# Attention into a spectral layer: early weights loaded as row pairs of two modes, and the spectrum moved on PE's queue

## The chip, the cores and the metric

The kernel runs on one core of one Trainium2 chip. A core has a matrix engine (TensorE, "PE" in the profile, its weight loads "PEld"), three engines for element-wise work (VectorE "DVE", ScalarE "ACT", GpSimd "POOL"), a synchronising engine (SyncE, "SP") and 16 DMA engines that move data between HBM and the on-chip memory SBUF. Each engine works through a queue of its own in order and waits at semaphores. Matmul results go to a second memory, PSUM, which is divided into banks.

The metric is the device time of one execution in microseconds (us), as a median of several runs.

## What is computed

The first half is causal attention with a decay that comes from a gate `f`; the second a layer that multiplies the first 64 Fourier modes of the sequence by complex matrices, adds the result back, and applies a channel matrix with a ReLU. Cut to the core:

```python
scores = (q @ k.T) / sqrt(64) + cum[:, None] - cum[None, :]   # cum = cumsum(log(clip(f)))
attn   = softmax(where(causal, -1e9, scores))
x      = concat_heads(attn @ v)                # [8, 576, 512]
X      = rfft(x, axis=1)[:, :64]
Yr     = Xr @ w_r[m] - Xi @ w_i[m]             # for each mode m, [512, 512] matrices
Yi     = Xr @ w_i[m] + Xi @ w_r[m]
u      = x + irfft(Y, n=576)
out    = u + relu(u @ w_ch)
```

Batch 8, 8 heads of 64 channels, sequence 576. The two weight tensors hold 64 x 512 x 512 float32 numbers each, 134 MB in all; DMA reads them as float32 and writes them to SBUF as bfloat16.

## The kernel before

**Two stages.** Attention runs over 32 pairs of heads, `pairs[i] = (g, b)`: g (0 to 3) is a block of 128 channels, b the batch. The loop at L588 makes 34 passes; each issues loads for pairs ahead and then interleaves pair i's scores with pair i - 1's product with v and pair i - 2's Fourier transform. The main loop (L835) then goes over 16 units u of four modes each and finishes the product with the mode matrices; inverse transform, channel matrix and stores follow. The order of the instructions is the order in which the code emits them: nothing reorders them.

**A pass of the attention loop** on PE: scores in three tiles (L457, bank `sps`), v's transposes (`turn_v`, L404, tile `tv`), products with v of the pair before (`av`, L505, `pav`), transposes of q and k of the next pair (L377, `tp`), a last score block whose exponential is `e` (L451), the last block of `av`, v's transposes back (`back_v`, L415, `vp`), then the Fourier transform `dft` of pair i - 2 (L536 or L557, `pd`). ACT takes the exponentials `et` (L464), the copy `vs` of v (L426) and the copies out of `pd`. DVE copies transposed q, k and v (L382, L406), normalises (`rcp` L519, `x_all` L520), applies masks (L470, L473, `m` L474) and scales v for the next pair (`vn`, L394). Setup work is emitted in passes 0 to 9: the Fourier basis `bas3` in pass 1 (`setup_basis`), small constants in pass 2 (`setup_late`), the inverse basis in 3 to 9 (`bip`).

**Units and blocks.** A unit's weights for one block `dc` of input channels are 1 MB in bfloat16. Blocks are loaded in the order `wseq` (L128): blocks 0 and 1 of units 0 to 7 (`by_rows`, 16 of them), block 0 of units 8 to 15, block 1 of units 8 to 11, and the rest in the main loop. For `by_rows` a block holds w_r and w_i of 128 channels, one row of 512 numbers in a packet. For the other units a block holds w_r (dc = 0) or w_i (dc = 1) of 256 channels as row pairs, 1024 numbers in a packet. Blocks live in seven buffers of `wpool` and, for seven of them, as guests in parts of `x_all` and `yx` that are free then (L136). Attention issues half blocks, two in a pass and one in passes 3, 6, 9, 12 and 15 (`less`). 28 blocks are used within attention (`spec_early`): two in each of passes 10 to 13 and 17 to 19, one in each of 20 to 33. A block's use is `spec_mms`: eight matmuls of 512 columns into one bank `A`. There, four modes stand side by side in four groups of 32 output columns of PE (rows 32j of `A`). The result is copied to `yacc` by ACT (block 0) or added by DVE (block 1).

**Spectrum.** `dft` multiplies x of pair i (576 rows in four blocks of 128 and one of 64) by `bas3` with three copies c of the basis (-imaginary, real, imaginary). For g < 2, the modes below 32 go to `XS`, 24 numbers (c, b) for each mode, all 128 channels; the modes from 32 go to `XQ` for even and odd channels, in the half of partitions that belongs to g. That is three groups of five matmuls and two copies on ACT. For g of 2 or 3 two groups of five write `XP`.

**Loads.** Weights, q, k and v are issued from POOL's queue (L112, L122, L167, L176, L185), stores from SP's. A load waits for its buffer and for the landing of the load that was issued eight loads before on this queue.

## Time and profile before

| | |
|---|---|
| median of 3 runs | 437.46 us (435.47 to 437.74) |
| the profiled execution | 436.07 us, span 434.2 us |
| granted TensorE clock, mean | 0.947 |
| PE busy | 360.4 us, 83% of the span |
| DVE busy | 265.7 us, 61% |
| ACT busy | 229.0 us, 53% |
| POOL busy | 141.0 us, 32% |
| DMA | 96.79 MB in 60,289 packets; 28,752 of them under 2 KB |
| HBM | 163.73 MB read, 9.44 MB written |

The profile is one execution; all its times count from the span's start. The page cuts the span into 40 equal slices (10.9 us each) and prints a digit for each engine, the busy share in tenths, 9 for 90% or more. GB/s counts the bytes written by DMA: a weight is read at 4 bytes and written at 2. The DMA share in a table of stretches is the sum of the packets' times over 16 engines, and packets overlap, so it stands above 1 when the engines are busy throughout. Recorded times of a matmul hold its way through the pipeline, so neighbours overlap: what a group costs PE is the time to the next group's start.

### The profile page before, as it was taken

How to read it: one execution, taken by the hardware profiler on the slowest of the kernel's cores; microseconds unless marked ns; L12 is line 12 of the kernel's file. 1: busy time of each engine (PE TensorE's matmuls, PEld its weight loads, DVE VectorE, ACT ScalarE, POOL GpSimd, SP SyncE). 2: the span in 40 equal slices, each digit the busy share in tenths (PEclk: the TensorE clock that was granted, in tenths of full speed). 3: DMA queues.
4: the chain of work that ended last, by engine and by line, in shares of the span. 5: the costliest groups of instructions: out<-in, count | busy, mean ns of one | idle time of the engine just before them, and what ended most of it. 6: DMA issues, size and time to landing. Idle time of an engine off the chain costs nothing.

```text
span 434.2 us, 10695 instructions
## 1 busy us (share of the span) xinstructions
PE 360.4 (83%) x4433; PEld 200.9 (46%) x4444; DVE 265.7 (61%) x651; ACT 229.0 (53%) x374; POOL 141.0 (32%) x211
## 2 busy tenths in 40 slices
PE   1699999988898899999986386599788599989993
PEld 1466666655665565665653133244343233334330
DVE  6687888776878797787785122222323157654794
ACT  4656667677775567667661022033313176652783
POOL 6544445434544434444304101111111112001273
PEclk9999999999999999999999579599969699999997
DMA  9999999999999999999999999999999999996598
GB/s 193 205 234 220 232 222 232 226 229 230 231 231 228 230 230 230 230 230 229 236 214 212 212 212 212 212 213 212 212 212 212 212 212 212 211 212 126 188 381 305
DMA packets 60289, 96.79 MB, mean 223 GB/s; under 512 B 3664, under 2 KB 28752, under 8 KB 60240
## 3 DMA queue, kind: packets, MB, share of 16 engines
q0 software_dynamic: 54544, 85.63, 103.6%
q1 hardware_dynamic: 5696, 10.47, 6.7%
q8 instruction: 35, 0.57, 0.5%
q14 instruction: 14, 0.11, 0.1%
HBM read 163.73 MB, written 9.44 MB: 399 GB/s over the span
## 4 chain that ended last, share of the span: by engine, by line
DMA 49%; PE 31%; DVE 9%; ACT 5%; issue 3%; POOL 1%; DVEq 0%; ACTq 0%; POOLq 0%
DMA w<-in_moe_w_i_dram 34%; DMA w<-in_moe_w_r_dram 13%; PE pd L536 5%; PE pav L505 5%; PE sps L457 5%; DVE qkT L382 4%; PE tv L404 3%; ACT et L464 2%; PE A L221 2%; PE pd L557 2%; DVE vT L406 2%; PE tp L377 2%; DMA qk<-in_k_dram 2%; DVE x_all L520 2%; PE U L692 2%
## 5 line engine op out<-in xcount | busy, mean ns | idle before, releaser
L464 ACT ACTIVATE et<-sps 128x1024 bf16<-128x1024 f32 x96 | 93.2, 1023 | 11.6 <-PE sps L457 9.7
L505 PE MATMUL pav<-vs,et 128*128 128x65 bf16 (+1 forms) x896 | 51.3, 197 | 14.6 <-ACT e L451 14.3
L505 PEld LDWEIGHTS <-et 128*128 128x128 bf16 (+1 forms) x896 | 39.9, 103 | 34.0 <-issue 31.7
L382 DVE COPY qkT<-tp 128x640 bf16<-128x640 bf16 x64 | 48.9, 765 | 3.4 <-PE tp L377 3.4
L892 DVE TENSOR_TENSOR Yb<-A,yx 128x512 bf16<-128x512 f32 x15 | 10.4, 692 | 59.0 <-PE A L221 59.0
L406 DVE COPY vT<-tv 128x576 bf16<-128x576 bf16 x32 | 24.2, 757 | 35.4 <-PE tv L404 34.7
L732 PE MATMUL pxw<-wch,xT 128*128 128x512 bf16 (+1 forms) x152 | 41.1, 418 | 1.0 <-DVE xT L722 0.4
L457 PE MATMUL sps<-qkT 64*128 64x512 bf16 (+4 forms) x320 | 39.4, 310 | 1.3 <-DVE qkT L382 1.1
L426 ACT COPY vs<-vp 128x576 bf16<-128x576 bf16 x32 | 20.4, 639 | 37.1 <-PE vp L422 37.1
L520 DVE TENSOR_TENSOR x_all<-pav,rcp 128x384 bf16<-128x384 f32 (+2 forms) x96 | 36.2, 377 | 3.3
L221 PE MATMUL A<-w,XP 128*16 128x512 bf16 (+1 forms) x240 | 21.3, 435 | 20.2 <-DMA w<-in_moe_w_i_dram 12.1
L377 PE MATMUL tp<-ident_bf,qk 128*64 128x128 bf16 x576 | 30.1, 235 | 9.3 <-DMA qk<-in_k_dram 9.0
L185 POOL DMA_DIRECT2D w<-in_moe_w_r_dram x16 | 11.9, 743 | 74.6 <-PE A L221 69.2
L739 ACT CAST XW<-pxw 128x512 bf16<-128x512 f32 (+1 forms) x16 | 9.4, 585 | 45.2 <-PE pxw L732 45.2
L739 ACT CAST yx<-pxw 128x512 bf16<-128x512 f32 (+1 forms) x24 | 14.0, 585 | 33.9 <-PE pxw L732 33.9
L782 ACT CAST x_all<-pu 128x512 bf16<-128x512 f32 (+1 forms) x40 | 23.4, 585 | 13.1 <-PE pu L775 12.2
L112 POOL DMA_DIRECT2D qk<-in_q_dram x32 | 19.5, 609 | 30.8 <-PE tp L377 6.5
L185 POOL DMA_DIRECT2D w<-in_moe_w_i_dram x19 | 13.3, 698 | 50.0 <-PE A L221 40.5
L732 PEld LDWEIGHTS <-xT 128*128 128x128 bf16 (+1 forms) x160 | 15.8, 109 | 22.9 <-issue 9.6
L722 DVE COPY xT<-ptr 128x576 bf16<-128x576 bf16 x32 | 14.7, 458 | 17.8 <-PE ptr L717 17.0
L112 POOL DMA_DIRECT2D qk<-in_k_dram x32 | 19.2, 601 | 19.1 <-DMA w<-in_moe_w_i_dram 5.9
L377 PEld LDWEIGHTS <-qk 128*64 128x64 bf16 x576 | 19.5, 116 | 12.7 <-issue 8.2
(158 smaller groups left out, 703.3 us busy)
## 6 DMA issues: line engine op xcount, KB each, us to landing
w<-in_moe_w_i_dram POOLq DMA_DIRECT2D x19, 1024.0 KB, 31.9
w<-in_moe_w_r_dram POOLq DMA_DIRECT2D x16, 1024.0 KB, 29.9
w<-in_moe_w_r_dram POOLq DMA_DIRECT2D x23, 512.0 KB, 11.3
w<-in_moe_w_i_dram POOLq DMA_DIRECT2D x19, 512.0 KB, 11.0
out_dram<-o_sb SPq DMA_DIRECT2D x36, 256.0 KB, 2.8
vt<-in_v_dram POOLq DMA_DIRECT2D x29, 288.0 KB, 10.4
qk<-in_q_dram POOLq DMA_DIRECT2D x32, 144.0 KB, 10.7
qk<-in_k_dram POOLq DMA_DIRECT2D x32, 144.0 KB, 10.7
```

What stands on the lines that cost most here:

```text
L112: nc.gpsimd.dma_start(qk[64 * n : 64 * n + 64, :, :], src[b, 2 * g : 2 * g + 2, :, :].rearrange("h (p r) d -> p h (r d)", p=64),)
L185: nc.gpsimd.dma_start(w8[:, j : j + step, :, :].rearrange("p m r e -> p m (r e)"), src[m : m + step, 256:512, :].rearrange("m (p r) e -> p ...
L221: nc.tensor.matmul(A[32 * j : 32 * j + M, :], lhsT=lhsT, rhs=rhs, start=st_, stop=sp_)
L377: nc.tensor.transpose(tp[64 * hp : 64 * hp + 64, r - r0, :, :].rearrange("p n c -> p (n c)"), qk[:, hp, r * 64 : r * 64 + 64], ident_bf[:, :],
L382: nc.vector.tensor_copy(st[i]["T"][:].rearrange("p n (c r) -> p n c r", r=9)[:, :, :, r0:r1], tp[:, 0 : r1 - r0, :, :].rearrange("p r n c ...
L406: nc.vector.tensor_copy(st[i]["vT"][:].rearrange("p (c r) -> p c r", r=9), tv[:].rearrange("p r c -> p c r"))
L457: nc.tensor.matmul(ps[:, hp, c : c + n], lhsT=KT[sl, jb * 128 : jb * 128 + 128], rhs=QT[sl, i0 : i0 + n], start=True, stop=True,)
L464: nc.scalar.activation(st[i]["et"][:, T, :, :], ps[:], ACT.Exp, scale=scale)
L505: nc.tensor.matmul(pav[:Ms, sb % 3, hp, :], lhsT=eblk(i, hp, jb, sb), rhs=rhs, start=(jb == 0), stop=(jb == sb),)
L520: nc.vector.tensor_tensor(x_all[:ns, g, b, lo:hi, :].rearrange("p s (h d) -> p s h d", h=2), pav[:ns, lo % 3 : lo % 3 + n, :, 0:Dh], _stri ...
L732: nc.tensor.matmul(pxw[rows, :], lhsT=xT[:, eb, sb * 128 : sb * 128 + Ms], rhs=wch[:, eb, :], start=(eb == 0), stop=(eb == NEB - 1),)
L739: nc.scalar.copy(XW[to][rows, sb, :], pxw[rows, :])
```

## The change

Four things are done together.

1. The `by_rows` blocks are loaded as row pairs: partition 2p + h holds rows 2p and 2p + 1 of modes 4u + 2h and 4u + 2h + 1 (h is 0 or 1), w_r and w_i after one another, 1024 numbers in a packet. The other blocks of dc < 2 are loaded in two halves of 128 channels, into the even and the odd partitions; in the main loop, where a block was one load, it is now two (four blocks).
2. A `by_rows` block's eight matmuls go to two groups of 64 or 48 output columns instead of four of 32. Each multiplies the two modes of both partition parities at once; the spectrum holds zeros where the parity doesn't match. The spectrum of dc = 0 is `XS`, that of dc = 1 lies in a part of `yx`; in both the modes (16) are innermost, so that a matmul's stationary operand has a step of 16 elements.
3. `dft` for g < 2 takes x of all channels, of the channels moved by one up, and by one down (`x_pad` has 32 zeros ahead of x for it): three groups of five matmuls with 192, 48 and 144 columns (g = 1: 192, 144, 48) instead of 96 each. The copies: two on ACT with a factor per partition that is 1 or 0 by parity, 96 elements each; and `XQ` by one ACT copy of 192 elements for g = 0 (all partitions), by two additions on DVE for g = 1.
4. `dft(i - 2)` is emitted ahead of `back_v(i)` instead of after the first early unit.

`bas3` is written with its modes in another order, by nine instructions on DVE instead of three, with a reduction for the parity and eight memsets. Some constants (`m_i`, `m_f`, `rep`) move into `XP`'s place, and the guests in `yx` start at other offsets.

```diff
         if by_rows(u, dc):
             for t, src in enumerate((moe_w_r, moe_w_i)):
                 if half in (None, t):
                     nc.gpsimd.dma_start(
-                        w8[:, t, :, :],
-                        src[4 * u : 4 * u + 4, dc * 128 : (dc + 1) * 128, :].rearrange("m p e -> p m e"),
+                        w8[:, 2 * t : 2 * t + 2, :, :].rearrange("p k r e -> p k (r e)"),
+                        src[4 * u : 4 * u + 4, dc * 128 : (dc + 1) * 128, :].rearrange(
+                            "m (p r) e -> p m (r e)", r=2
+                        ),
                     )
         elif dc < 2:
             src = (moe_w_r, moe_w_i)[dc]
-            step = 4 if half is None else 2
-            for j in range(2 * (half or 0), 4 if half != 0 else 2, step):
-                m = 4 * u + j
-                nc.gpsimd.dma_start(
-                    w8[:, j : j + step, :, :].rearrange("p m r e -> p m (r e)"),
-                    src[m : m + step, 0:256, :].rearrange("m (p r) e -> p m (r e)", r=2),
-                )
+            for g in range(2):
+                if half in (None, g):
+                    nc.gpsimd.dma_start(
+                        w8[g:128:2, :, :, :].rearrange("p m r e -> p m (r e)"),
+                        src[4 * u : 4 * u + 4, 128 * g : 128 * g + 128, :].rearrange(
+                            "m (p r) e -> p m (r e)", r=2
+                        ),
+                    )
...
     def spec_mms(A, u, dc, first, last):
         w8 = wtile.pop((u, dc))
+        if by_rows(u, dc):
+            for t in (1, 0):
+                for r in range(2):
+                    for k in range(2):
+                        M = 64 if t else 48
+                        c0 = 16 * (56 * r + (0 if t else 8)) + 2 * u + k
+                        nc.tensor.matmul(
+                            A[64 * k : 64 * k + M, :],
+                            lhsT=by_mode(dc)[:, c0 : c0 + 16 * M - 15 : 16],
+                            rhs=w8[:, 2 * t + k, r, :],
+                            start=first and t == 1 and r == 0,
+                            stop=last and t == 0 and r == 1,
+                        )
+            return
...
     def dft(i):
         g, b = pairs[i]
         if g < 2:
-            pd = psM.tile([128, 3, 3, ML], F32, tag="m", name="pd")
-            half = slice(64 * g, 64 * g + 64)
-            for r in range(3):
+            pd = psM.tile([128, 3, 2 * NM], F32, tag="m", name="pd")
+            even, odds, upper = (16, 0, 32) if g == 0 else (48, 32, 0)
+            cut = 16 if g else 48
+            for o, m0, m1, at in (
+                (0, 0, NM, even),
+                (1, 0, cut, NM + even),
+                (-1, cut, NM, 0),
+            ):
                 for sc in range(NSB):
                     ns = SBLK[sc]
-                    xs = x_all[:ns, g, b, sc, :]
+                    M = 127 if o == 1 and sc == NSB - 1 else 128
+                    c0 = 32 + ((g * B + b) * NSB + sc) * 128 + o
                     nc.tensor.matmul(
-                        pd[half, r, :, :] if r else pd[:, 0, :, :],
-                        lhsT=xs[:, r - 1 : 128 : 2] if r else xs,
-                        rhs=bas3[:ns, sc, :, ML:NM] if r else bas3[:ns, sc, :, 0:ML],
+                        pd[:M, :, at : at + m1 - m0],
+                        lhsT=x_pad[:ns, c0 : c0 + M],
+                        rhs=bas3[:ns, sc, :, m0:m1],
                         start=(sc == 0),
                         stop=(sc == NSB - 1),
                     )
-            nc.scalar.copy(
-                XS[:, g, 0 : 24 * ML].rearrange("p (m c b) -> p c m b", c=3, b=8)[:, :, :, b],
-                pd[:, 0, :, :],
-            )
-            nc.scalar.copy(
-                XQ[half, :, :, :].rearrange("p r (c b) m -> p r c b m", c=3)[:, :, :, b, :],
-                pd[half, 1:3, :, :],
-            )
+            pr = pd[:].rearrange("p c (r m) -> p r c m", r=2)
+            for h, k in enumerate((even, odds)):
+                nc.scalar.activation(
+                    by_mode(g)[:, 0 : 16 * 112].rearrange("p (r c q) -> p r c q", r=2, q=16)[
+                        :, :, 32 * h + b : 32 * h + 24 : 8, :
+                    ],
+                    pr[:, :, :, k : k + 16],
+                    ACT.Copy,
+                    scale=odd[:, h : h + 1],
+                )
+            xq = XQ[:].rearrange("p r (c b) m -> p r c b m", c=3)[:, :, :, b, :]
+            up = pr[:, :, :, upper : upper + 32]
+            if g == 0:
+                nc.scalar.activation(xq, up, ACT.Copy, scale=odd[:, 0:1])
+            else:
+                for r in range(2):
+                    nc.vector.scalar_tensor_tensor(
+                        xq[:, r], up[:, r], odd[:, 1:2], xq[:, r], ALU.mult, ALU.add
+                    )
             return
...
             av(prev, 4)
+        if i >= 2:
+            dft(i - 2)
         if live:
             back_v(i)
...
             spec_done += 1
-        if i >= 2:
-            dft(i - 2)
```

## The prediction

> **What bounds the kernel now.** I read the page's slices first.

> ```profile
> PE   1699999988898899999986386599788599989993
> DMA  9999999999999999999999999999999999996598
> GB/s 193 205 234 220 232 222 232 226 229 230 231 231 228 230 230 230 230 230 229 236 214 212 212 212 212 212 213 212 212 212 212 212 212 212 211 212 126 188 381 305
> ```

> The DMA engines are busy in each slice up to about 394 us; only the last 40 us are without loads. So nothing can end earlier unless the loads take less time or are kept waiting less. Next I asked the DMA view for two stretches, 8 to 20 us (by_rows weights and q, k) and 260 to 300 us (weights as row pairs).

> ```profile
> DMA packets 2444, 2.46 MB, mean 205 GB/s; under 512 B 157, under 2 KB 2444, under 8 KB 2444
> ...
> DMA packets 4248, 8.48 MB, mean 212 GB/s; under 512 B 126, under 2 KB 126, under 8 KB 4245
> ```

> Packets of 1 KB move 205 GB/s, those of 2 KB 212. Then the table by stretches, for the engines (PE, PEld, DVE, ACT, POOL busy, clock, DMA share, GB/s).

> ```profile
> 30.00:60.00 30.00, 28.21 (x463) 19.59 (x461) 25.44 (x75) 19.72 (x34) 13.42 (x21) 1.00 1.21 228
> ...
> 180.00:220.00 40.00, 37.38 (x649) 24.91 (x649) 31.01 (x87) 27.12 (x41) 15.77 (x24) 1.00 1.13 230
> 260.00:300.00 40.00, 30.11 (x220) 14.20 (x223) 11.79 (x24) 8.78 (x15) 6.66 (x9) 0.87 1.12 212
> ```

> In attention (to about 229 us) PE is busy 94% too: two bounds lie close together. The loop over pairs runs at PE's, ACT's and DVE's pace; the loads run in a queue beside it. The queue is fed by POOL, and POOL's timeline at the end of attention shows how near they are.

> ```profile
> 216.15 0.74 POOL L185 DMA_DIRECT2D w<-in_moe_w_r_dram  x1 [5.05 <-PE AT L233]
> 222.66 0.74 POOL L185 DMA_DIRECT2D w<-in_moe_w_i_dram  x1 [5.77 <-PE A L221]
> 228.94 0.74 POOL L185 DMA_DIRECT2D w<-in_moe_w_r_dram  x1 [5.53 <-PE A L221]
> 231.76 0.74 POOL L185 DMA_DIRECT2D w<-in_moe_w_i_dram  x1 [2.08 <-PE A L221]
> ```

> There a load is issued when PE has used up an earlier weight and its buffer is free: one in 6.5 us, PE's pace, where DMA needs 4.95 us (1 MiB at 212 GB/s). What keeps DMA busy is the backlog. Counting bytes issued less bytes moved (the trace's packets), 1.82 MB are outstanding just before the issue at 228.94: 8.6 us at 212 GB/s. That is the least of these issues (9.9 to 11.6 us at the three beside it), so 8.6 us is the **cover**: if attention runs later by D, loads lose D − 8.6 us, and every later stage with them.

> Last, one pass of the loop, on PE (90 to 99 us) and on ACT (50 to 58 us).

> ```profile
> 90.88 1.37 PE L536 MATMUL pd<-bas,x_all 128*128 128x96 bf16 x15 [0.24 <-ACT vs L426]
> 92.18 0.61 PE L221 MATMUL A<-w,XS 128*32 128x512 bf16 x8
> ...
> 96.75 0.28 PE L505 MATMUL pav<-vs,et 128*64 128x65 bf16 x4 [0.72 <-ACT e L451]
> ...
> 97.16 0.40 PE L415 MATMUL vp<-ident_bf,vT 128*128 128x128 bf16 x4
> ```
> ```profile
> 50.47 0.22 ACT L451 ACTIVATE e<-pav 128x64 bf16<-128x64 f32 x1
> 52.09 0.64 ACT L426 COPY vs<-vp 128x576 bf16<-128x576 bf16 x1 [1.40 <-PE vp L422]
> 53.14 0.60 ACT L543 CAST XS<-pd 128x96 bf16<-128x96 f32 x1 [0.42 <-PE pd L536]
> 53.28 0.61 ACT L547 CAST XQ<-pd 64x192 bf16<-64x192 f32 x1
> 53.79 2.98 ACT L464 ACTIVATE et<-sps 128x1024 bf16<-128x1024 f32 x3
> 56.67 0.22 ACT L451 ACTIVATE e<-pav 128x64 bf16<-128x64 f32 x1
> ```

> The loop closes from `e` to `e` in 6.20 us: PE waits for `e`, does av's last block (0.41 to the next start), vp (0.47), pd (1.41), in five passes bip (0.26), first scores (0.32), hands over (0.17); ACT does three `et` and `e` (3.12). With 0.05 to start that is 5.95, with bip 6.21. Note that vs's copy is hidden behind pd.

> **The change part by part.**

> *Packets.* Sixteen units' 16,384 packets of 1 KB become 8,192 of 2 KB. A least-squares fit of the packets of each size in slices of 4 us, 8 to 392 us, gives 79.3 ns of an engine for 1 KB and 154.9 for 2 KB: 8,192 x (2 x 79.3 − 154.9) = 30 us over 16 engines, **−1.9 us** (by the two rates above −2.7, the far end; the other end 0). The other sixteen units now land in every second partition, 64 at a time, at the same packet size. No row has that step; q and k land in 64 neighbours, at 91.5 ns for 1,152 B, 3 to 4% above what the 1 KB packet gives per byte. So 0 to +3.2 us (4% of 16 x 4.95); I take 0. Four units in the main loop need a second issue, 0.74 us each on POOL, beside 25 to 30 us of backlog: nothing.

> [...] The two rates differ by 3%, so the measurement decides.

> *Early units on PE.* Eight matmuls of 512 columns today go to four 32-column groups, four side by side: 0.54 us to the next start. One pass of 512 columns takes 0.215 us (four pywl matmuls in a row, 0.86 in the chain of waits). Now they go to two groups of up to 64 columns. No row shows two such at 512 columns; if four still ran together +0, if one at a time +1.28. Nearest are the transposes into two 64-column halves (L377, ten of 128 columns in 0.45, less than 10 x 0.054), which overlap: two at a time, 0.97, **+0.43** for each of 16 units.

> [...]

> *Spectrum on PE.* Before, three groups of five matmuls with 96 columns: 1.37. L557's two groups with 192 columns take 1.35 (chain of waits). So a group is 0.457 at 96 and 0.675 at 192, 2.27 ns a column; now 192, 144 and 48: 0.675 + 0.566 + 0.348 = 1.59, **+0.22** a pair (ends: 1.3 if 128-column loads let it go faster, 1.9).

> *Copies.* XS's scattered 0.60 becomes two of 96 elements in runs of 16. Ends 0.23 (`e`, 64 elements) and 0.60; I take 0.25, nearest to `e`. XQ for g = 0 0.33. For g = 1 XQ becomes two DVE additions, 0.25 each (rcp 0.18, 128-element x_all 0.29).

> *Order.* On PE pd now stands ahead of vp; so on ACT the spectrum's copies stand ahead of vs, and the next pass's av and `et` stand behind vs. For g = 1 DVE's two additions wait for pd, and behind them stand rcp, x_all, mask, m and vn, for which PE's tv waits. Passes, `e` to `e`:

> - 2 to 9: 0.05 + 0.41 + 1.63 (pd to the next start) + 0.17 + ACT (0.25 + 0.25 + 0.33 + 0.64, less 0.08 overlap each) 1.2 + 3.12 = 6.58: +0.37 in five, +0.63 in three, 3.7.
> - 10 to 13, two units each, 7.61 now (pd to pd in the chain of waits, 83.27 to 90.88): 0.05 + 0.41 + 1.63 + 0.47 + 2 x 0.97 + 0.17 + yx copy 0.51 + 3.12 = 8.30: 2.8.
> - 14 to 16, 6.28 now (112.91 to 119.19): to pd's end 2.26, DVE chain to vn 2.17 (additions 0.50, vs column 0.16, rcp and x_all 0.15 + 0.29 + 0.15 + 0.28, mask 0.41, m 0.21, vn 0.74, less nine overlaps of 0.08), tv, av, tp, scores 1.41, 0.17, one `et` and `e` 1.13 = 7.14: 2.6.
> - 17 to 21: the first with two units 0.05 + 0.41 + 1.63 + 0.47 + 1.94 + 0.32 + 0.17 + 3.12 = 8.11, 0.53 over its 7.58; 18 and 19 are held by DVE's additions of A today (7.83), so I take half of the units' 0.86, 0.4 each; 20 and 21 with one unit and pd at 1.38 6.89 against 6.45, 0.44 each: 2.2.
> - 22 to 31, vs behind XP: about 0.1 each, 1.0.

> *Set-up on DVE in pass 1.* Nine basis copies, 3 x (0.31 + 2 x 0.24) = 2.4 in place of 3 x 0.47; a reduction (0.28, L282's size) and eight memsets (0.085 each): +1.8, less overlaps, 1.0.

> **Sum.** D = 1.0 + 3.7 + 2.8 + 2.6 + 2.2 + 1.0 = 13.3 us. Of these 8.6 are covered; DMA runs dry for the rest (and the 1.9 saved only make it dry sooner, so they are lost). The profiled execution took 436.07: 436.07 + 13.3 − 8.6 = 440.8. The runs shown lie from 435.47 to 437.74, median 437.46, so I add half the distance, 0.7: **441.5 us**.

> **Rivals.**

> 1. *The cover holds* (not slower). Place: the issues between 216 and 232 us. If D stays under 8.6 − 1.9 = 6.7 us, DMA never runs dry, and the time is 436.07 − 1.9 = 434.2, with the 0.7 434.9. For it: 7 us of D are PE's early units and 3.5 pd, and either at its low end brings D to 6 to 10; PE's 0.72 wait for `e` may swallow some. Against: three queues grow at once. It decides below D = 6.7.
> 2. *Halves one at a time*: +1.28 instead of 0.43 for 16 units, D = 13.3 + 16 x 0.85 = 26.9, 436.07 + 26.9 − 8.6 = 454.4, with the 0.7 455.1. The L377 row speaks against it.
> 3. *Stepped partitions cost DMA time.* At +3.2 us it is hidden as long as DMA runs dry anyway; with rival 1 it gives 434.9 + 3.2 = 438.1. Twice the price per packet would add 79 us; no row hints at that.
> 4. *The packets don't double* (a descriptor for each row after all): with D = 13.3 the time is the same 441.5, since the saving is lost anyway.

> **How the numbers follow.** Forecast 0.55, its own range 438 to 448 (D from 10 to 19); rival 1 0.30; rival 2 0.09; rival 3 0.05; rival 4 0.01. A measurement of this kernel can tell about 0.5% from no change: from 437.46 that is 435.3 to 439.6. Rival 1 lies at that edge: half of its chance counts as faster, half as the same; rival 3 and the low end of the forecast, 0.10 together, are the same, and the rest is slower: faster 0.15, same 0.25, slower 0.60. The range reaches from rival 1 to the forecast's far end, 434 to 450.

> **What would show it.** The page's packets under 2 KB should fall by 16,384, and the first slices rise from 205 to 212 GB/s where only weights and q, k move. pd should take about 1.6, A<-w,XS 0.97 to the next start, with vs in ACT's timeline behind three copies; `e` to `e` 6.6, 8.3 and 7.1 in the three kinds of pass. Between 210 and 245 us the DMA share should dip for 3 to 6 us in sum. I am wrong if DMA stays at 9 throughout with loads ending near 392 us (rival 1), or if the passes keep their length.

## The result and the profile after

The changed kernel takes 462.98 us (median of 4 runs, 459.39 to 465.01); the kernel before took 436.56 beside it (435.47 to 437.74). The ratio is 1.060, with a 95% interval of 1.052 to 1.067: 26 us slower, where the forecast was 4 us slower and the range ended at 450. The profiled execution took 462.97 us, span 461.1.

First the slices of the page of after (40 of 11.5 us each).

```profile
PE   1779988888888878999999878469889589989993
...
PEclk9995899999886577999999999759998969999997
DMA  8999999989989069999999989999999999999498
GB/s 192 212 230 222 233 233 235 236 153 232 222 165 180 9 118 230 226 236 223 235 237 204 185 156 212 212 212 211 212 212 212 211 212 211 211 213 211 150 382 308
DMA packets 52161, 96.80 MB, mean 210 GB/s; under 512 B 3728, under 2 KB 12432, under 8 KB 52112
```

The bytes are the same and the packets under 2 KB fell by 16,320 (16,384 fewer of 1 KB, 64 more under 512 B), so the loads are as predicted. Three things were not there before: holes in DMA in the middle of attention (one slice of 9 GB/s), a dent at attention's end (slices 22 to 24), and a granted clock below full inside attention. Before, the clock was full from 33.6 us to the end of attention. The table by stretches (us, then PE, PEld, DVE, ACT, POOL busy, clock, DMA share, GB/s), for before and then for after:

```profile
26.00:50.00 24.00, 22.88 (x367) 15.54 (x367) 20.34 (x63) 16.02 (x25) 10.24 (x17) 1.00 1.22 224
...
120.00:180.00 60.00, 53.42 (x918) 34.72 (x918) 48.62 (x128) 38.96 (x58) 26.16 (x41) 1.00 1.15 230
```
```profile
26.00:50.00 24.00, 21.11 (x270) 13.52 (x270) 16.89 (x61) 12.53 (x21) 10.13 (x16) 0.64 1.15 226
...
120.00:180.00 60.00, 49.70 (x590) 31.72 (x587) 33.45 (x93) 25.14 (x41) 16.58 (x27) 0.69 0.76 144
```

In the two stretches PE's busy time is 7 to 8% less than before, but it does 26 and 36% fewer matmuls (270 for 367, 590 for 918): its clock is at 0.64 and 0.69 there, where it was at 1.00.

The passes tell where the time went. Length of a pass from `e` to `e` (k is the pass that ends with pair k's `e`), read from the starts of `e` on ACT. The prediction numbers a pass by the one before: its 2 to 9 are 3 to 10 here, its 10 to 13 are 11 to 14, and so on.

| passes | before | after | lost | predicted |
|---|---|---|---|---|
| 2 (set-up) | 6.71 | 5.58 | -1.1 | 1.0 |
| 3, 4 | 6.56, 6.11 | 10.02, 9.55 | 6.9 | 3.7 with the next row |
| 5 to 10 | 6.04 to 6.27 | 6.80 to 6.92 | 4.1 | |
| 11 to 14 | 7.6 each | 8.84 three times, 10.41 | 6.5 | 2.8 |
| 15 to 17 | 6.3 each | 8.09, 9.46, 9.88 | 8.6 | 2.6 |
| 18 to 22 | 6.45 to 7.83 | 12.45, 13.52, 7.80, 6.94, 6.93 | 11.5 | 2.2 |
| 23 to 31 | 6.3 to 7.0 | 6.2 to 6.8 | -1.0 | 1.0 |

The last `e` starts at 260.9 us in place of 225.5: D, its lateness, is 35.4 us, not 13.3. And 436.07 + 35.4 - 8.6 = 462.9, the measured 462.97: the sum's frame held, and its largest term was wrong.

POOL's timeline shows the hole of DMA. First the load of unit 9's first half in before, then the same stretch of after:

```profile
136.13 0.72 POOL L176 DMA_DIRECT2D yx<-in_moe_w_r_dram  x1 [1.73 <-DMA w<-in_moe_w_i_dram]
```
```profile
143.03 0.62 POOL L180 DMA_DIRECT2D yx<-in_moe_w_r_dram  x1
146.20 0.60 POOL L117 DMA_DIRECT2D qk<-in_q_dram  x1 [2.54 <-PE tp L425]
...
165.01 0.64 POOL L180 DMA_DIRECT2D yx<-in_moe_w_r_dram  x1 [17.60 <-DVE yx L647]
```

Unit 9's first half, a guest in yx, waits 17.6 us for DVE's sums of two early units. These lie in row 0 of yx, the guest in rows 5 to 7. Behind it in POOL's queue wait all the other loads.

Two full-clock passes, one on PE (with two units, g = 1) and one on ACT (g = 0), for the single costs:

```profile
91.75 1.58 PE L590 MATMUL pd<-bas,x_pad 128*128 128x192 bf16 x15
93.26 0.40 PE L463 MATMUL vp<-ident_bf,vT 128*128 128x128 bf16 x4
...
94.59 1.14 PE L236 MATMUL A<-x_pad,XS 128*64 128x512 bf16 x8 [0.79 <-ACT vs L474]
95.46 1.15 PE L236 MATMUL A<-w,XS 128*64 128x512 bf16 x8
```
```profile
59.10 0.57 ACT L599 ACTIVATE XS<-pd,odd 128x96 bf16<-128x96 f32 x2 [2.08 <-PE pd L590]
59.56 0.42 ACT L610 ACTIVATE XQ<-pd,odd 128x192 bf16<-128x192 f32 x1
59.87 0.65 ACT L474 COPY vs<-vp 128x576 bf16<-128x576 bf16 x1
```

pd takes 1.51 to the next start (I had 1.59 to 1.63), a unit 0.87 to 1.07 (0.97), the XS copies 0.57 the pair and XQ 0.42 (0.50, 0.33). Each operation was priced about right. Not seen: the 0.79 us for which the first unit waits for a bank. The row names `vs`, whose copy ends at 94.55. But DVE's additions to XQ, the last to read pd, end at 94.52, and a version below, in which they go ahead of ACT's copies, tells the two apart:

```profile
97.66 1.14 PE L242 MATMUL A<-x_pad,XS 128*64 128x512 bf16 x8 [0.82 <-ACT yx L612]
```

There ACT's two copies of pd end at 97.61 and `vs` only at 98.14. So the unit takes over pd's bank, and waits for whichever engine reads pd last.

### The profile page after: what moved, and what is told of

Same layout as the page of the kernel before. It is cut to its first block, busy times and chain, and to the rows that moved or that the text cites. A ratio compares the mean times of both kernels' runs of the same rounds, so it can differ in the third digit from the quotient of the medians.

```text
span 461.1 us, 10729 instructions
## 1 busy us (share of the span) xinstructions
PE 382.4 (83%) x4433; PEld 217.3 (47%) x4444; DVE 271.9 (59%) x681; ACT 228.1 (49%) x382; POOL 140.0 (30%) x215
## 4 chain that ended last, share of the span: by engine, by line
DMA 38%; PE 32%; issue 11%; ACT 8%; DVE 6%; POOL 3%; DVEq 0%; POOLq 0%; ACTq 0%
DMA w<-in_moe_w_i_dram 19%; DMA w<-in_moe_w_r_dram 16%; PE pd L590 6%; PE A L236 5%; PE pav L553 5%; PE sps L505 3%; ACT et L512 3%; PE tp L425 2%; PE tv L452 2%; DMA qk<-in_k_dram 2%; DMA yx<-in_moe_w_r_dram 2%; PE U L757 2%; PE Z L757 1%; POOL w L191 1%; PE U L1022 1%
## 5 line engine op out<-in xcount | busy, mean ns | idle before, releaser
L512 ACT ACTIVATE et<-sps 128x1024 bf16<-128x1024 f32 x96 | 94.3, 1025 | 33.6 <-PE sps L505 31.6
L553 PE MATMUL pav<-vs,et 128*128 128x65 bf16 (+1 forms) x896 | 53.7, 202 | 12.3 <-ACT e L499 10.2
L553 PEld LDWEIGHTS <-et 128*128 128x128 bf16 (+1 forms) x896 | 42.4, 107 | 33.1 <-issue 25.6
L505 PE MATMUL sps<-qkT 64*128 64x512 bf16 (+4 forms) x320 | 41.9, 329 | 1.2 <-DVE qkT L430 1.1
L425 PE MATMUL tp<-ident_bf,qk 128*64 128x128 bf16 x576 | 31.6, 244 | 10.1 <-DMA qk<-in_k_dram 8.9
L797 PE MATMUL pxw<-wch,xT 128*128 128x512 bf16 (+1 forms) x152 | 39.2, 403 | 0.9 <-DVE xT L787 0.4
L568 DVE TENSOR_TENSOR x_pad<-pav,rcp 128x384 bf16<-128x384 f32 (+2 forms) x96 | 36.2, 377 | 3.5
L117 POOL DMA_DIRECT2D qk<-in_q_dram x32 | 19.8, 619 | 42.9 <-PE tp L425 35.5
L847 ACT CAST x_pad<-pu 128x512 bf16<-128x512 f32 (+1 forms) x40 | 23.4, 585 | 13.3 <-PE pu L840 12.4
L191 POOL DMA_DIRECT2D w<-in_moe_w_i_dram x19 | 13.3, 699 | 54.5 <-PE A L250 38.1
L590 PE MATMUL pd<-bas,x_pad 128*128 128x192 bf16 (+7 forms) x240 | 29.0, 246 | 0.7 <-DVE qkT L430 0.7
L127 POOL DMA_DIRECT2D vt<-in_v_dram x29 | 16.7, 576 | 30.4 <-DVE vn L442 19.6
L442 DVE TENSOR_TENSOR vn<-vt,wn 128x576 bf16<-128x576 f32 x32 | 23.8, 744 | 2.1 <-ACT wn L348 2.1
```

The lines of the kernel that those rows point to most:

```text
L191: nc.gpsimd.dma_start(w8[:, j : j + step, :, :].rearrange("p m r e -> p m (r e)"), src[m : m + step, 256:512, :].rearrange("m (p r) e -> p ...
L425: nc.tensor.transpose(tp[64 * hp : 64 * hp + 64, r - r0, :, :].rearrange("p n c -> p (n c)"), qk[:, hp, r * 64 : r * 64 + 64], ident_bf[:, :],
L442: nc.vector.tensor_tensor(vn[:], st[i]["vt"][:], _strided(wn[:, widx(i), :], [[1, 9], [0, Dh]]), ALU.mult)
L505: nc.tensor.matmul(ps[:, hp, c : c + n], lhsT=KT[sl, jb * 128 : jb * 128 + 128], rhs=QT[sl, i0 : i0 + n], start=True, stop=True,)
L512: nc.scalar.activation(st[i]["et"][:, T, :, :], ps[:], ACT.Exp, scale=scale)
L553: nc.tensor.matmul(pav[:Ms, sb % 3, hp, :], lhsT=eblk(i, hp, jb, sb), rhs=rhs, start=(jb == 0), stop=(jb == sb),)
```

## The experiments

All times are beside runs of before on the same chip: 435.67, 436.02, 436.10 and 435.73 us in the four sets. "Last e" counts from the span's start, as in the table, and is that of the profiled execution. Gains are differences of medians; each median of a slower version is good to some 1 to 3 us (its 95% interval), and against before on the same chip some gains come out up to 0.9 us smaller. Three causes are tested: the order on PE's queue ("order theory"), the wait of the stepped loads in POOL's queue ("load theory"), and half clock brought by PE's waits, first by those for DVE's set-up ("clock theory").

**The causes one at a time, from after.** Order back:

```diff
-        if i >= 2:
-            dft(i - 2)
         if live:
             back_v(i)
...
             spec_early(*early[spec_done])
             spec_done += 1
+        if i >= 2:
+            dft(i - 2)
```

> After with one edit: the spectrum of pair i-2 stands again behind v's transposes back and the first early unit, as before. Order theory: pd ahead of vp costs most of the lost passes; by my hand-laid schedule D falls by about 8 us (35.5 to 27), passes 5 to 10 go from 6.87 to 6.2-6.4 and 11 to 13 from 8.84 to 8.3, and the time is near 455. Rival (clock and load theories): the half clock from 32 to 49 us and the dry DMA from 150 to 165 us stay, order only moves waits about, and the time stays at 460 to 463.

Measured 447.20 us (1.0266, 1.0244 to 1.0287), last e 244.7. Passes 5 to 10 at 6.34 to 6.41, 11 to 14 at 8.24 to 8.31, 15 to 17 at 6.04, below before; 18 and 19 still at 13.13 and 15.36. The order is worth 16 us here, twice what I gave it, and the wait in POOL's queue stays (13.5 us).

Two tiles for yx:

```diff
-    yx = const.tile([128, 8, 1280], F32, name="yx")
+    yx = const.tile([128, 4, 1280], F32, name="yx")
+    yh = const.tile([128, 4, 1280], F32, name="yh")
...
-        return yflat[:, 9216 : 9216 + XROW // 2].bitcast(BF16)
+        return XPf[:, 512 + 4 * KL : 512 + 4 * KL + XROW]
```

> After with yx cut into two tiles (rows 0 to 3, rows 4 to 7) and the lower modes' second spectrum moved out of it into XP, which is written only later. Load theory: a load into every second partition of a shared tile waits for everything the program did with that tile before, so with a tile of their own units 16 and 17 are issued near 137 to 145 us, POOL has no 17.6 us wait on DVE, DMA does not fall to 9 GB/s, passes 18 and 19 take at most 8.8 us (before this edit 12.5 and 13.5), and the time falls by 8 to 10 us to 453-455. Rival: the wait is only a symptom of late passes; then POOL waits elsewhere and the time stays above 460.

Measured 453.90 (1.0405, 1.0378 to 1.0432); passes 18 and 19 at 9.22 and 7.86 (I had said 8.8 at most), POOL's wait gone. The statement that XP is written only later was wrong: from pass 18 on the spectra of g = 2 overwrite parts of the second spectrum, so units 2 to 7 multiply a partly overwritten spectrum in this version, and their weight loads wait for copies to XP (0.3 us at most). I repeated it below in a form without that.

Basis ahead of the loop. In after, PE waits here behind DVE's set-up:

```profile
30.80 0.41 PE L425 MATMUL tp<-ident_bf,qk 128*64 128x128 bf16 x8 [0.90 <-DVE vT L454]
...
32.22 2.38 PE L590 MATMUL pd<-bas,x_pad 128*128 128x192 bf16 x15 [0.72 <-DVE qkT L430]
```

```diff
+    setup_basis()
     less = (3, 6, 9, 12, 15)
...
-        if i == 1:
-            setup_basis()
```

> After with the whole basis set-up moved from pass 1 to ahead of the loop, where DVE is idle from 6.1 to 8.9 us. Clock theory: PE's waits of 0.90 and 0.72 us near 30 us, which DVE's 2.3 us of basis copies make, bring the half clock of 32 to 49 us; without them the clock stays full until at least 100 us, passes 3 and 4 take 6.9 in place of 10.0 and 9.6, and the time falls by about 6 us to 457. Rival: PE's smaller waits in every later pass bring the half clock anyway; then an episode of over 10 us appears before 100 us and the time stays at 460 to 463.

Measured 461.44 (1.0576, 1.0545 to 1.0607). The half clock of 32 to 49 us is gone and passes 3 and 4 take 6.80 and 6.87, as the clock theory has it. But the clock now falls for 3.4 us in each of passes 11 to 14, which take 10.3 to 10.45 in place of 8.84 (14 had 10.41 already): what was won is given back, and the time is within the scatter of after's. Both theories are half right.

**The same causes put into before.** Its basis written twice in pass 1 (`setup_basis()` called twice):

> Before with its basis written twice in pass 1 (the same values, 1.4 us more on DVE, about what after adds there). Clock theory: PE waits about 1 us near 31 to 33 us and then runs at half clock for some 10 to 17 us, so the last e comes 4 to 7 us later (225.7 to 230-233); the cover of 8.6 us takes that, so the time stays at 436 to 437.5. Rival: a wait of this length leaves the clock alone; then the last e comes at most 1.5 us later, and the time is 436 as well. If the cover is not there, the time grows by what e is late, to 440 or more.

Measured 435.81 (1.0002, 0.9989 to 1.0016). PE's timeline of this version:

```profile
31.45 0.41 PE L377 MATMUL tp<-ident_bf,qk 128*64 128x128 bf16 x8 [1.05 <-DVE vT L406]
...
32.87 0.58 PE L415 MATMUL vp<-ident_bf,vT 128*128 128x128 bf16 x4 [0.73 <-DVE qkT L382]
33.84 2.02 PE L536 MATMUL pd<-bas,x_all 128*128 128x96 bf16 x15 [0.19 <-DVE qkT L382]
```

Two waits of 1.05 and 0.73 us, and pd takes 2.02 in place of 1.51: the clock records are at half from 32.6 to 39.4 us. Pass 3 takes 9.68. The last e is 2.4 us late, less than the 4 to 7 expected (pass 2 is 1.1 us shorter, as the clock had come up at 25.7 in place of 33.6), and the time does not move: the cover is real.

The order alone in before (`dft` ahead of `back_v`):

> Before with the order alone: the spectrum of pair i-2 ahead of v's transposes back. Order theory: 0.3 to 0.6 us more in passes 5 to 10, and 1 to 3 us more in each of 14 to 17, where PE has no early units to run while it waits; last e 6 to 14 us later, time from 436 (cover holds) to 441. Rival: the order only hurts together with the wider pd and the longer copies; then the passes stay within 0.2 us of before, and the time is 435.7.

Measured 436.93 (1.0016, 1.0002 to 1.0030), last e 231.6: 6.1 late and nearly covered. Passes 5 to 8 cost 0.33 to 0.43 more, 9 and 14 to 17 0.5 to 1.7, with the clock at half for 3.4 us at 73, 111, 121 and 128; 19 and 20 are shorter than before (7.11 for 7.83).

The packets alone:

```diff
-                        w8[:, t, :, :],
-                        src[4 * u : 4 * u + 4, dc * 128 : (dc + 1) * 128, :].rearrange("m p e -> p m e"),
+                        w8[:, t, :, :].rearrange("p (k r) e -> p k (r e)", r=2),
+                        src[4 * u : 4 * u + 4, dc * 128 : (dc + 1) * 128, :].rearrange(
+                            "m (p r) e -> p m (r e)", r=2
+                        ),
```

> Before with the first sixteen units' weights loaded as row pairs of two modes by partition parity, 2 KB a packet, and nothing else changed: the sums of these units are of the wrong rows. DMA is busy throughout, so the time shows the packets alone: 1.9 us less by the fit of packet times (433.8), 2.7 less by the two rates, 0 if 1 KB packets lose nothing.

Measured 433.90 (0.9952, 0.9934 to 0.9970): 2.1 us (1.3 to 2.9 by the interval), against 1.9 by the fit and 2.7 by the two rates: both are possible, 0 is not.

The stepped loads alone (the code of after's L180 in place of L176):

> Before with the loads of the other sixteen early units (u from 8, rows 0 to 255) into every second partition, 64 at a time, as after has them, and nothing else changed: these units' sums are of the wrong rows. If stepping partitions costs DMA nothing and the wait of the units in yx is harmless at the pace of before: 435.7. If stepping costs 4% of their time: up to 3.2 us more, 438.9. If the load theory holds here too: POOL waits 8 us or more for DVE at unit 17, DMA falls under 100 GB/s for a slice, passes 18 and 19 grow by some us each, and the time grows by 2 to 10 us.

Measured 440.30 (1.0096, 1.0072 to 1.0120). POOL's timeline of this version:

```profile
131.51 0.62 POOL L175 DMA_DIRECT2D yx<-in_moe_w_r_dram  x1
...
145.49 0.64 POOL L175 DMA_DIRECT2D yx<-in_moe_w_r_dram  x1 [10.22 <-DVE yx L583]
```

The wait appears with this edit alone, passes 18 and 19 take 17.76 and 11.97, and 201.97 + 240.4 (time before less its last e and the cover, plus the new last e) is 442.4, the profiled execution's time. In slices beyond the hole DMA moves 227 to 235 GB/s as before: stepping costs the transfers nothing that shows, the wait costs all.

**All of it undone but the loads.** Order back, yx in two tiles and basis early together:

> After with all three edits: order back, yx in two tiles with the second spectrum in XP, basis ahead of the loop. If the three causes add up as they showed alone: passes 5 to 10 at 6.4, 11 to 14 at 8.3, 15 to 17 at 6.04, 18 at 8.6 or less, the last e about 6 us later than before (231 to 232), less than the cover of 8.6 us, so DMA never runs dry; then the time is that of before, 435.7, less what the doubled packets save: 433.8 by my estimate of 1.9 us, 435.7 if they save nothing. Rival: a fourth cause is left (width of the units and of pd), the last e is over 8.6 us late and the time is above 437.

Measured 435.68 (0.9993, 0.9976 to 1.0010), last e 232.3. No half clock in attention, passes 5 to 17 as expected, but 18 to 22 longer, with PE waiting 0.56 us for the copy to XP in each of 21 and 22; that is the overwritten spectrum named above, in the same units. The last e is 6.8 us late, under the rival's 8.6, and the time far from its 437; but of the packets' 1.9 us next to nothing shows.

So the loads of the two units in yx were made another way, without a step over partitions, yx left as after has it:

```diff
+            for j in range(4) if n in guests else ():
+                if half in (None, j // 2):
+                    nc.gpsimd.dma_start(
+                        w8[:, j, :, :].rearrange("p r e -> p (r e)"),
+                        src[4 * u + j, 0:256, :].rearrange("(g p r) e -> p g (r e)", g=2, r=2),
+                    )
```

With order back and basis early:

> After with order back, basis ahead of the loop, and the loads of the two units that lie in yx made without stepping partitions, a mode at a time into all 128; yx stays one tile and the second spectrum stays in it. If the second spectrum in XP made the waits of 0.56 us that PE had ahead of the first-spectrum units in passes 18 to 22 of the version with all three edits: these waits are gone, passes 18 to 22 take 7.9, 7.9, 8.5, 7.0 and 7.0, the last e is about 4 us later than before (229 to 230), DMA never runs dry and the time is 433.8 to 434.3, the packets' saving. Rival: the late last e has another cause (pd's width, the units); then it stays over 231.5 and the time at 435 to 436.

Measured 435.03 (0.9975, 0.9958 to 0.9992), last e 231.5. The waits for XP are gone (20 to 22 as expected), but 18 and 19 take 8.81 and 8.54, so the last e is later than I said, at the rival's 231.5, and DMA still runs short for two slices:

```profile
PEclk9999999999999999999999789589996689999997
DMA  8999999999999999999999999999999999998597
GB/s 180 208 238 222 237 224 235 232 232 233 236 233 225 234 226 234 227 232 228 237 212 182 197 212 212 212 212 212 211 212 212 211 211 212 212 212 164 201 378 295
```

These are the rows of its page: no hole in attention, full clock until its end, and 182 and 197 GB/s after it.

The same with the spectra of passes 18 and later left ahead, where the order is a gain:

> The same, but the spectra of passes 18 and later (pairs 16 to 31) stay ahead of v's transposes back, as in after, where the order gained 0.1 to 0.7 us a pass. Last e 1.5 to 2.5 us earlier than without this edit; if DMA is never dry in either, the time is the same, 433.8 to 434.3; if that kernel still runs dry at 215 to 245 us, this one is faster by up to 1.5 us.

Measured 434.64 (0.9976, 0.9953 to 1.0000), last e 228.0, 3.5 us earlier. It and the version above take 1.1 to 1.5 us off before (this one's interval reaches 1) and 28 off after; their difference is within the scatter.

**What the order costs, and why.** After with the two loads whole and nothing else:

> After with only the loads of the two units in yx changed (all 128 partitions, a mode at a time). Load theory, now with the spectrum left where after has it: no POOL wait on DVE over 3 us, DMA not under 150 GB/s in any slice of attention, passes 18 and 19 at 8 to 9, last e at 246 to 249, time 451 to 454.

Measured 455.35 (1.0386, 1.0326 to 1.0446): the wait's removal is worth 7.6 us. POOL's longest wait on DVE is 3.7 us. Pass 19 is at 7.85 as expected, but 14 to 18 are at 8 to 12.3 with the clock at half from 131.7 to 162.4, so the last e (252.5) and the time are beyond what I said. And with the basis early as well, so that only the order is left:

> After with the two loads in yx made whole and the basis ahead of the loop: of the three causes only the order is left. Order theory: passes 5 to 10 still 6.8 to 6.9 and 14 to 17 8 to 9.9 with half clock there, though DMA is never dry; last e 12 to 18 us later than before, time 439 to 446. Rival: the half clock in passes 14 to 17 came from the dry DMA; then 14 to 17 take 7.1 to 7.6, the last e is 8 to 10 us late and the time 436 to 438.

Measured 454.26 (1.0415, 1.0376 to 1.0453), against 435.03 with the order back: 19.2 us for the order alone, and 8 us over the range that I gave. DMA is not quite "never dry" (113 GB/s in one slice), but now as a consequence: POOL waits for q's and v's buffers (up to 3.7 us at a time), which late passes release. Pass 15 shows the mechanism. DVE's timeline, then PE's:

```profile
123.38 0.54 DVE L619 SCALAR_TENSOR_TENSOR XQ<-pd,odd,XQ 128x96 bf16<-128x96 f32 x2 [1.69 <-ACT yx L605]
...
125.17 0.74 DVE L448 TENSOR_TENSOR vn<-vt,wn 128x576 bf16<-128x576 f32 x1
```
```profile
121.15 1.58 PE L596 MATMUL pd<-bas,x_pad 128*128 128x192 bf16 x15
...
124.07 0.35 PE L559 MATMUL pav<-vs,et 128*128 128x65 bf16 x6 [0.54 <-DVE rcp L573]
...
125.96 0.47 PE L458 MATMUL tv<-ident_bf,vn 64*64 64x64 bf16 x18 [1.22 <-DVE vn L448]
...
129.32 2.43 PE L596 MATMUL pd<-bas,x_pad 128*128 128x192 bf16 x15
```

pd ends at 122.73, just where the prediction put it (2.26 after `e`), but DVE's additions start at 123.38: they wait for ACT's two copies of the same bank, not for pd alone. PE waits 0.54 and 1.22 us; of the 3.41 us up to 127.4 it is busy for 61% (see the last section), and from there the clock is at half (pd 2.43 for 1.58) for 30.7 us: 16 to 18 take 9.88, 9.88 and 12.43. Two runs take the two links apart. DVE's additions issued ahead of ACT's copies (the loop over `scalar_tensor_tensor` moved above the one over `nc.scalar.activation`):

> The version with only the order left, and in it DVE's two additions to XQ issued ahead of ACT's two copies of the same bank (they wait for ACT's second copy there, 0.6 to 0.7 us after pd's end). Queue theory: DVE's queue (rcp, x_pad, masks, vn) starts some 0.6 us earlier in passes 10 to 17, PE's wait for vn in pass 15 falls from 1.22 to about 0.6 us, the busy share of that window rises over 70%, and the half clock of 127 to 158 us shrinks or goes; passes 15 to 17 take 7.2 to 7.5 in place of 7.9, 9.9 and 9.9 and the time falls by 4 to 8 us to 446-450. Rival: the wait for vn has other causes (ACT's vs, the masks); then passes 15 to 17 change by less than 0.5 us each and the time stays at 453 to 455.

Measured 442.55 (1.0152, 1.0112 to 1.0192). DVE's timeline now:

```profile
123.03 0.54 DVE L608 SCALAR_TENSOR_TENSOR XQ<-pd,odd,XQ 128x96 bf16<-128x96 f32 x2 [1.09 <-PE pd L596]
```

Now ACT waits for DVE, and then PE for ACT:

```profile
123.67 0.57 ACT L612 ACTIVATE yx<-pd,odd 128x96 bf16<-128x96 f32 x2 [2.72 <-DVE vs L479]
```
```profile
124.82 0.34 PE L559 MATMUL pav<-vs,et 128*128 128x65 bf16 x6 [1.03 <-ACT vs L480]
...
125.62 0.47 PE L458 MATMUL tv<-ident_bf,vn 64*64 64x64 bf16 x18
```

So the wait for the shared bank has changed sides rather than gone. DVE's queue is 0.6 us earlier, ACT's copies later, and PE waits 1.03 us once, for `vs`, in place of 0.54 and 1.22; its wait for `vn` is gone. The window up to 127.4 is 71% busy in place of 61%, and the clock stays full. Passes 15 to 18 are at 7.34, 7.34, 7.81 and 9.25, with half clock only from 141.0 to 144.5. In all this was worth 11.7 us, more than I gave it. And work added on PE, with the additions left behind the copies:

```diff
         tv = psM.tile([128, 9, 64], BF16, tag="m", name="tv")
+        if 14 <= i < 18:
+            for _ in range(20):
+                nc.tensor.transpose(
+                    tv[:, 0:2, :].rearrange("p r c -> p (r c)"), ident_bf[:, :], ident_bf[:, :]
+                )
```

> The version with only the order left, with 20 transposes of the identity more on PE ahead of v's transposes in passes 14 to 17, into the bank that the real ones overwrite (about 1.1 us of work a pass at full clock, where PE waits for vn). Clock theory: the added work keeps PE's windows over 80% busy, the clock stays full from 25 to 230 us, passes 15 to 17 fall from 7.9, 9.9, 9.9 to about 8 each or less and 18 from 12.4 to 9, so more work makes the kernel 5 to 9 us faster (445 to 449). Rival: these passes are long by their queues, not by the clock; then they grow by up to 1 us each and the time is 454 to 457.

Measured 446.56 (1.0244, 1.0207 to 1.0281): 80 transposes more, 7.7 us less. PE's timeline of pass 15 in it:

```profile
126.49 1.29 PE L457 MATMUL tv<-ident_bf 128*128 128x128 bf16 x20
127.78 0.47 PE L463 MATMUL tv<-ident_bf,vn 64*64 64x64 bf16 x18
...
130.90 1.58 PE L601 MATMUL pd<-bas,x_pad 128*128 128x192 bf16 x15
```

The filler stands where PE waited for vn. Pass 15 keeps its 7.94 and 16 to 18 fall to 7.94, 8.07 and 8.84: the next pd is back at 1.58. The clock is full from 99.7 us to the end of attention. Against the expectation 12 and 14 grew: 14 by the filler itself (10.07), since PE does not wait there, and 12 (10.27) by a half clock of 3.4 us at 96, ahead of the filler.

## Why the prediction was wrong

The direction and the frame were right, the size of D was not. By its steps:

- **What bounds the kernel, and the cover: right.** Beyond 8.6 us of lateness the time grows with the last e: 201.97 + last e gives 462.9, 442.4 (stepped loads in before), 444.4 (filler) and 441.8 (additions first), measured in the profiled executions at 462.97, 442.45, 444.82 and 442.31; the largest miss among all versions is 2.3 us. Below it little is lost, if not nothing: 2.4 us late gave 435.8, and 6.1 late 436.9, 0.9 over before (0.1 to 1.3). With the packets doubled, 6.0 us late left 1.1 of their 2.1 us by the medians and two slices at 182 and 197 GB/s, where the prediction had DMA never dry up to 6.7. What DMA missed in the middle of attention is not added on top.
- **Packets, -1.9 us: right in size** (2.1 alone, in before, within 1.3 to 2.9), and lost in after, as the step said. The rate from 8 to 20 us rose only to 206 GB/s, not to 212. The interval of the run with the packets alone (0.9934 to 0.9970) does not hold 1.
- **Loads into every second partition.** "No row has that step ... So 0 to +3.2 us" looked at the transfers alone. (91.5 ns for 1,152 B is 2.6% above the 1 KB packet for each byte, not 3 to 4; the term was taken as 0.) The failed part is that such a load into a tile shared with other data waited for earlier work on other rows of that tile: 17.6 us in POOL's queue, about 7.6 us of time in after, 4.3 in before. I asked what a wait would hold up in the queues of ACT and DVE, and not whether a load gets a new one.
- **Early units and pd on PE: right for each, too high in sum** (7 and 3.5 us by the prediction). With order, loads and basis undone, what is left is 0.1 to 0.3 us in passes 4 to 10, 0.7 in 11 to 14, where two units and the wider pd lie, nothing in 15 to 17, and 0.5 to 1.2 in 18 to 22: 6.0 us in all with pass 2, which is 1.3 shorter as the clock came up earlier. Halves one at a time (rival 2) and packets that don't double (rival 4) fall with these rows and the packet count, rival 3 with the rate in the stepped run, rival 1 with D.
- **The order: this is the step that failed.** "14 to 16 ... = 7.14: 2.6" had DVE's additions wait for pd; they wait for ACT's two copies as well, and pass 15 is 7.94 at full clock. "10 to 13 ... 2.8" missed the unit's wait of 0.79 us for pd's bank. Above all every pass was added up at full clock. With only the order left, half clock followed PE's waits of 0.54 and 1.22 us, and there PE is the bound, 77 to 100% busy in each window from 127.4 to 158.1: passes 16 and 17 took 9.88 where 7.14 was forecast. Put back in after, the order brings 15.8 us, and 19.2 with the other two causes undone; alone in before, where it has the cover, it costs 0.9.
- **Set-up, 1.0 us: right on DVE, wrong on what follows.** DVE is 1.03 us longer at it (27.79 to 30.01 in place of 27.92 to 29.11). But the waits that it makes on PE (0.90 and 0.72 us) were followed by half clock for 17.07 us, which the version with the basis early does not have, and passes 3 and 4 lose 6.9. Undone alone, the set-up brings 1.5 us, less than the scatter of after's runs: the clock falls later instead.

Undone one after the other, the wait of the stepped loads is worth 7.6 us, the basis 1.1 (not told from 0 by these runs) and the order 19.2: 27.9 of 462.98, which leaves 435.03, the packets' saving in part (1.1 of 2.1 us). The shares hold for this sequence alone: undone first, the order brings 15.8 us and the wait of the loads, by two tiles, 9.1.

## What to carry to other kernels

Before a longer queue is priced by adding up durations, ask what share of PE's time its waits leave: here 1.3 us of waiting in 3.4 was followed by half clock in the next three passes, and filling such waits with useless work was worth 7.7 us. An instruction's waits are read also from what it shares with others (a bank that another engine reads, 0.65 us for DVE's additions in pass 15; a tile that other data lie in, 17.6 us for unit 9's load), not only from the data that it needs. And in a queue in order, such as POOL's here, one load that waits holds all the loads behind it: in after DMA fell to 9 GB/s in one slice.

## What the runs showed of the hardware

| window ends at (us) | PE busy in it | PE's waits that lie in it, whole or in part | half clock after it |
|---|---|---|---|
| 32.3 | 1.79 us, 52% | 0.90 and 0.72 us for DVE's set-up | 17.07 us |
| 121.0 | 2.47 us, 72% | 0.39 us for `e`, 0.79 for pd's bank | 3.41 us |
| 134.7 | 1.88 us, 55% | 0.54 us for `rcp`, 1.22 for `vn` | 3.41 us |
| 141.5 | 2.38 us, 70% | 0.54 us for `rcp`, 1.22 for `vn` | 23.89 us |
| 172.2 | 1.46 us, 43% | 3.48 us for a load into yx | 6.83 us |

The other 48 windows at full clock in after's attention (25.5 to 261.0 us) were 77 to 100% busy, and full clock followed each. In before all 57 from 33.6 to 228.1 us were followed by full clock, at 71 to 100% busy. Of the 16 windows at half clock in after's attention, the five that were followed by full clock were 97 to 100% busy, the 11 others 55 to 100%.

So in these two profiles each fall came after PE had waited for 28 to 57% of a window, but two windows of before with PE waiting for 28 and 29% (up to 91.6 and 228.1 us) were followed by none. In the version with only the order left, the window that ended at 127.4 us was 61% busy, and half clock followed. No run shows at what share the clock changes; the shares here are those of recorded matmuls.

Where the windows lie in the passes differs between the profiles (full clock came at 33.56 us in before and at 25.46 in after, 2.4 windows apart), and so part of this may be luck. Passes 11 to 14 do the same work in the version with only the basis early and in the one with only the order left. In the first the clock fell in each of the four (10.3 to 10.45 us a pass), in the second in none (8.84). After itself has both: the windows with the unit's wait for pd's bank in passes 11 to 13 (up to 97.1, 104.0 and 114.2 us) were 77% busy and full clock followed, that of pass 14 was 72% busy and half clock followed (10.41).
